# A decode-attention kernel on one core: weight loads in two head halves, K/V transfers in pairs, softmax statistics in a ring

## The chip, the cores and the metric

The kernel runs on one core of one Trainium2 chip. The metric is the device time of one execution in microseconds (us). Runs of one kernel agree within about 1%; all runs quoted here are fast (none lies over 1.5% above the fastest of its kernel). A ratio is the mean time of one kernel's fast runs over the mean of the other's fast runs of the same rounds, so it is not quite the ratio of the medians that are quoted beside it.

Engines: PE is the matmul engine (PEld its weight loads), DVE the vector engine, ACT the scalar engine, POOL the GpSimd engine, SP the engine that issues DMA.

## The reference

Two independent attention blocks, A and B, each one decode step against its own cache; the outputs are joined. bf16 throughout.

```python
# B=8 sequences, D=1024, H=32 heads, Sk=4096 cached keys, Dh=128; twice, for A and B
q = (x @ wq).reshape(B, 1, H, Dh).transpose(0, 2, 1, 3)
scores = einsum("bhqd,bhkd->bhqk", q, k_cache) * Dh ** -0.5
p = softmax(scores, axis=-1)
o = einsum("bhqk,bhkd->bhqd", p, v_cache)
out = o.transpose(0, 2, 1, 3).reshape(B, 1, H * Dh) @ wo
```

2 x 8 x 32 = 512 pairs of cache and head are 512 *units*. Each needs 1 MB of K and 1 MB of V; with the weights, 1107 MB are read.

## The kernel before

Every operation is recorded in a graph (engine, emitter, dependencies, guessed duration, priority). A greedy list scheduler then fixes one order for each engine, in its own model of time:

```python
def _schedule(ops, cfg):
    SEM_LAT = cfg.get("sem_lat", 0.15)
    DMA_US_PER_MB = cfg.get("dma_us_per_mb", 2.72)
    ...                                  # among the operations that are ready, on all engines:
                key = (st, op.prio, op.idx, st)   # earliest modelled start, then priority
```

In a quarter of the units ("P") PE transposes K and does the scores; in the others ("D") DVE multiplies, adds and reduces. After the scores every unit goes through the same softmax chain:

```python
            o1 = g.add("dve", lambda e: e.tensor_reduce(rmax[:, u:u + 1], src, AX.X, ALU.max), [opScore[u]], 0.22, f"rmax{u}", prio - 0.5)
            o2 = g.add("pool", lambda e: e.partition_all_reduce(gmax[:, u:u + 1], rmax[:, u:u + 1], 128, bass.bass_isa.ReduceOp.max),
                       [o1], 0.45, f"armax{u}", prio)
            o3 = g.add("pool", lambda e: e.tensor_scalar(negb[:, u:u + 1], gmax[:, u:u + 1], -scale, None, ALU.mult),
                       [o2], 0.22, f"negb{u}", prio)
            o4 = g.add("act", lambda e: e.activation(pT[:, u % PR, :], src, ACTF.Exp, bias=negb[:, u:u + 1],
                                                     scale=scale, accum_out=rsum[:, u:u + 1]),
                       [o3, opPV.get(u - PR)], 0.42, f"exp{u}", prio - 0.5)
            ...
            if b == B - 1:               # last unit of a head: add the sums over the partitions
                opAradd[(c, h)] = g.add("pool", lambda e, ua0=ua0: e.partition_all_reduce(Lall[:, ua0:u + 1], rsum[:, ua0:u + 1], 128, bass.bass_isa.ReduceOp.add), ...)
```

I call the all-reduce of the maximum **G**, the tiny scale after it **n**, and the all-reduce of a head's sums **L**. All three run on POOL. Note that the model prices G at 0.45 us and n at 0.22 us.

The K, V and weight transfers:

```python
            opK[u] = dma(K_sb[:, kslot, :], caches[c][1][b, h].rearrange("(m t) d -> m (t d)", t=T), ("k", kslot), [opKfree.get(u - NK)], ...)
            opV[u] = dma(V_sb[:, vslot, :], caches[c][2][b, h].rearrange("(m t) d -> m (t d)", t=T), ("v", vslot), [opPV.get(u - NV)], ...)
        ...
        W_sb = sb("W_sb", [128, WSZ], BF16)      # WSZ = max(DC * HD, H * D): a whole weight matrix
```

## Time and profile before

| | before |
|---|---|
| time, median of 16 runs | 8114.6 us (8095 to 8135) |
| profiled span | 8100.5 us |
| time per unit | 15.8 us |
| busiest engine | DVE, 29% |
| DMA | 36% of 16 engines, 137 GB/s |

First the page of the kernel before: busy time with the share of the span, and the DMA queue with packets, MB and share.

```profile
PE 2257.7 (28%) x11890; PEld 940.4 (12%) x11890; DVE 2309.2 (29%) x1833; ACT 1035.8 (13%) x1893; POOL 614.6 (8%) x1106
...
q1 hardware_dynamic: 158272, 1107.43, 35.6%
...
issue 66%; DVE 17%; PE 8%; POOL 5%; ACT 2%; POOLq 0%; DMA 0%; SPq 0%; DVEq 0%
```

Nothing is busy even a third of the time, and two thirds of the chain that ended last are "issue": time in which an engine waited for nothing that the profile shows. So look for who waits, not for who works. The table of waits of the kernel before (engine, line and tile, what released it; us in total, times, longest):

```profile
ACT pT L419 <- POOL negb L417: 5810.5, 480, 21.9
PEld sc L435 <- ACT pT L419: 5110.6, 359, 32.2
...
POOL negb L417 <- issue: 4314.1, 479, 12.2
...
POOL gmax L415 <- issue: 1756.1, 289, 11.1
...
DVE prod L393 <- ACT qbc L552: 42.8, 18, 12.0
```

The exponential waits for n, PE waits for the exponential, and POOL, the engine with the least work, waits for "issue" in front of n and G. DVE's multiply waits 42.8 us in all, and that for qbc, not for K. The serial chain on POOL sets the pace; the question is what POOL does in those gaps. The views by source line of the kernel before answer it (op and count; duration in ns min/median/max; first and last start):

```profile
L417 POOLq MODIFY_POOL_CONFIG  x958: 82/83/83, 46.4 to 8081.5; - x192
L417 POOL TENSOR_SCALAR negb<-gmax x512: 209/261/2248, 56.8 to 8088.8; 128x1 f32<-128x1 f32 x171
...
L415 POOLq MODIFY_POOL_CONFIG  x832: 11/11/11, 14.6 to 8074.7; - x167
L415 POOL PARTITION_ALL_REDUCE gmax<-rmax x512: 352/379/2490, 45.2 to 8081.1; - x171
...
L426 POOLq MODIFY_POOL_CONFIG  x128: 11/11/11, 168.1 to 8089.4; - x128
```

What the trace shows is two MODIFY_POOL_CONFIG records in front of every change from G or L to n or back, and none between two instructions of one kind (G and L count as one kind). 958 records are 479 changes before n, 832 are 416 before G (one of them ahead of the first G), 128 are 64 before L. The records are 11 or 83 ns long; the time is in the gap behind them, never under 5.4 us in this trace. I call such a change, with its records and its gap, a *swap*; the recorded texts call it a reload. What POOL does in the gap is shown by no trace here. The timeline of POOL alone shows the rhythm (start, duration, instruction, and in brackets the idle time before it):

```profile
4054.68 0.26 POOL L417 TENSOR_SCALAR negb<-gmax 128x1 f32<-128x1 f32 x1 [9.17 <-issue]
4060.82 0.38 POOL L415 PARTITION_ALL_REDUCE gmax<-rmax  x1 [5.89 <-issue]
4068.41 0.26 POOL L417 TENSOR_SCALAR negb<-gmax 128x1 f32<-128x1 f32 x1 [7.21 <-issue]
4074.71 0.38 POOL L415 PARTITION_ALL_REDUCE gmax<-rmax  x1 [6.03 <-issue]
```

From start to start that is 6.1 and 6.3 us from n to G and 7.6 us from G to n, for instructions that report 0.26 and 0.38 us. So I time POOL from start to start.

### The profile page before, as it was taken

How to read it: one execution, taken by the hardware profiler on the slowest of the kernel's cores; microseconds unless marked ns; L12 is line 12 of the kernel's file. 1: busy time of each engine (PE TensorE's matmuls, PEld its weight loads, DVE VectorE, ACT ScalarE, POOL GpSimd, SP SyncE). 2: the span in 40 equal slices, each digit the busy share in tenths (PEclk: the TensorE clock that was granted, in tenths of full speed). 3: DMA queues.
4: the chain of work that ended last, by engine and by line, in shares of the span. 5: the costliest groups of instructions: out<-in, count | busy, mean ns of one | idle time of the engine just before them, and what ended most of it. 6: DMA issues, size and time to landing. Idle time of an engine off the chain costs nothing.

```text
span 8100.5 us, 32499 instructions
## 1 busy us (share of the span) xinstructions
PE 2257.7 (28%) x11890; PEld 940.4 (12%) x11890; DVE 2309.2 (29%) x1833; ACT 1035.8 (13%) x1893; POOL 614.6 (8%) x1106
## 2 busy tenths in 40 slices
PE   2222322222222222222222223222232222222223
PEld 1111111111111111111101111111111111111111
DVE  3232322323232233232222323223233232232322
ACT  1011111111111111111111111111111111111111
POOL 0000000000000000000000000000000000000000
PEclk7565565656556665656656665555565666566566
DMA  5433433333333333333343334333343333333332
GB/s 236 177 126 131 156 123 128 134 135 145 120 140 125 135 151 119 145 115 144 146 156 135 125 135 156 124 126 134 124 156 125 135 125 142 138 125 135 125 145 88
DMA packets 158431, 1109.50 MB, mean 137 GB/s; under 512 B 16928, under 2 KB 16928, under 8 KB 25152
## 3 DMA queue, kind: packets, MB, share of 16 engines
q1 hardware_dynamic: 158272, 1107.43, 35.6%
q8 instruction: 94, 1.54, 0.1%
q14 instruction: 65, 0.53, 0.0%
HBM read 1107.33 MB, written 0.03 MB: 137 GB/s over the span
## 4 chain that ended last, share of the span: by engine, by line
issue 66%; DVE 17%; PE 8%; POOL 5%; ACT 2%; POOLq 0%; DMA 0%; SPq 0%; DVEq 0%
DVE prod L393 7%; DVE s_sb L409 7%; PE sc L435 6%; POOL gmax L415 4%; DVE prod L403 3%; POOL negb L417 1%; PE sc L378 1%; ACT pT L419 1%; DVE rmax L414 1%; ACT KT_sb L367 1%; ACT accS L444 1%; PE misc L514 0%; POOLq L417 0%; PE kt_all L357 0%; POOL Lall L426 0%
## 5 line engine op out<-in xcount | busy, mean ns | idle before, releaser
L435 PE MATMUL sc<-V_sb,pT 128*4 128x512 bf16 x4096 | 1654.8, 577 | 5377.8 <-ACT pT L419 4962.7
L435 PEld LDWEIGHTS sc<-V_sb,pT 128*4 128x4 bf16 x4096 | 414.2, 111 | 6372.7 <-ACT pT L419 5110.6
L409 DVE TENSOR_REDUCE s_sb<-prod 128x32 f32<-128x2048 bf16 x382 | 872.8, 2285 | 719.1 <-ACT pT L419 708.6
L393 DVE TENSOR_TENSOR prod<-K_sb,qbc 128x4096 bf16<-128x4096 bf16 x382 | 871.7, 2282 | 42.8 <-ACT qbc L552 42.8
L414 DVE TENSOR_REDUCE rmax<-sc 128x1 f32<-128x32 f32 x130 | 24.7, 190 | 2612.2 <-PE sc L378 2612.2
L495 DVE RECIPROCAL rl<-Lall 128x8 f32<-128x8 f32 x64 | 13.0, 203 | 2261.3 <-POOL Lall L426 2261.3
L419 ACT ACTIVATE pT<-s_sb,negb 128x32 bf16<-128x32 f32 x382 | 122.7, 321 | 4167.9 <-POOL negb L417 4167.9
L415 POOL PARTITION_ALL_REDUCE gmax<-rmax x512 | 379.9, 747 | 2770.1 <-issue 1756.1
L417 POOL TENSOR_SCALAR negb<-gmax 128x1 f32<-128x1 f32 x512 | 202.2, 395 | 4316.7 <-issue 4314.1
L367 ACT ACTIVATE KT_sb<-kt_all 128x2048 bf16<-128x2048 bf16 x260 | 480.3, 1869 | 124.8 <-PE kt_all L357 124.4
L403 DVE TENSOR_TENSOR prod<-prod 128x2048 bf16<-128x2048 bf16 x382 | 467.8, 1225 | 9.7
L444 ACT ACTIVATE accS<-sc 4x512 bf16<-4x512 f32 x512 | 301.1, 588 | 1052.8 <-PE sc L435 1047.5
L357 PE MATMUL kt_all<-ident,K_sb 128*128 128x128 f32 x2080 | 329.3, 315 | 0.0
L357 PEld LDWEIGHTS kt_all<-ident,K_sb 128*128 128x128 f32 x2080 | 278.0, 165 | 119.0 <-issue 119.0
L419 ACT ACTIVATE pT<-sc,negb 128x32 bf16<-128x32 f32 x130 | 37.3, 287 | 1643.1 <-POOL negb L417 1642.7
L378 PE MATMUL sc<-QB,KT_sb 128*128 128x64 bf16 x4160 | 190.2, 215 | 133.1 <-ACT KT_sb L367 132.2
L378 PEld LDWEIGHTS sc<-QB,KT_sb 128*128 128x128 bf16 x4160 | 173.0, 113 | 206.3 <-ACT KT_sb L367 168.6
L452 PE MATMUL o_ps<-E,accS 128*128 128x4 bf16 x512 | 33.2, 169 | 185.9 <-ACT accS L444 185.8
L414 DVE TENSOR_REDUCE rmax<-s_sb 128x1 f32<-128x32 f32 x382 | 68.8, 180 | 10.6
L419 ACT ACTIVATION_READ_ACCUMULATOR pT<-s_sb,negb 128x1 f32 x382 | 71.1, 186 | 0.0
L552 ACT ACTIVATE qbc<-misc 128x512 bf16<-128x512 f32 x96 | 56.9, 593 | 69.2 <-PE misc L545 56.8
L545 PE MATMUL misc<-ident,qT_sb 128*128 128x128 bf16 x382 | 44.9, 251 | 57.8 <-ACT qbc L552 43.2
(39 smaller groups left out, 233.7 us busy)
## 6 DMA issues: line engine op xcount, KB each, us to landing
K_sb<-in_A_k_cache_dram SPq DMA_DIRECT2D x256, 1024.0 KB, 6.9
V_sb<-in_A_v_cache_dram SPq DMA_DIRECT2D x256, 1024.0 KB, 4.8
K_sb<-in_B_k_cache_dram SPq DMA_DIRECT2D x256, 1024.0 KB, 6.9
V_sb<-in_B_v_cache_dram SPq DMA_DIRECT2D x256, 1024.0 KB, 4.8
W_sb<-in_A_wq_dram SPq DMA_DIRECT2D x8, 1024.0 KB, 12.0
W_sb<-in_B_wq_dram SPq DMA_DIRECT2D x8, 1024.0 KB, 13.7
W_sb<-in_A_wo_dram SPq DMA_DIRECT2D x8, 1024.0 KB, 13.6
W_sb<-in_B_wo_dram SPq DMA_DIRECT2D x8, 1024.0 KB, 13.7
```

The source lines that it names most:

```text
L357: last = e.transpose(kt_all[:, gg, tt * 128:(tt + 1) * 128], K32[:, kslot, tp * 128:(tp + 1) * 128], ident32[:])
L367: return e.activation(KT_sb[:, pi % 2, lo * 1024:hi * 1024], ktb_all[:, lo:hi, :].rearrange("p g c -> p (g c)"), ACTF.Copy)
L378: last = e.matmul(bank[:, 2 * tp:2 * tp + MW], KT_sb[:, pi % 2, tp * 256 + e_:(tp + 1) * 256:2], QB[:, c, (j * 2 + e_) * 2:(j * 2 + e_) * ...
L393: lambda e: e.tensor_tensor(pv_, K_sb[:, kslot, :].rearrange("p (t d) -> p t d", d=Dh), qbc[:, gi % 2, i, :].unsqueeze(1).to_broadcast([12 ...
L403: lambda e, width=width: e.tensor_tensor(pv_[:, :, 0:width], pv_[:, :, 0:width], pv_[:, :, width:2 * width], ALU.add),
L409: lambda e, width=width: e.tensor_reduce(s_sb[:, di % SR, :], pv_[:, :, 0:width], AX.X, ALU.add),
L414: o1 = g.add("dve", lambda e: e.tensor_reduce(rmax[:, u:u + 1], src, AX.X, ALU.max), [opScore[u]], 0.22, f"rmax{u}", prio - 0.5)
L415: o2 = g.add("pool", lambda e: e.partition_all_reduce(gmax[:, u:u + 1], rmax[:, u:u + 1], 128, bass.bass_isa.ReduceOp.max), [o1], 0.45, f" ...
L417: o3 = g.add("pool", lambda e: e.tensor_scalar(negb[:, u:u + 1], gmax[:, u:u + 1], -scale, None, ALU.mult), [o2], 0.22, f"negb{u}", prio)
L419: o4 = g.add("act", lambda e: e.activation(pT[:, u % PR, :], src, ACTF.Exp, bias=negb[:, u:u + 1], scale=scale, accum_out=rsum[:, u:u + 1] ...
L435: last = e.matmul(pbank[32 * q4:32 * q4 + 4, 0:512], pT[:, u % PR, 4 * gq:4 * gq + 4], V_sb[:, vslot, gq * 512:(gq + 1) * 512], start=(gq ...
L444: opAcc[u] = g.add("act", lambda e: e.activation(accS[32 * q4:32 * q4 + 4, ring, :], pbank[32 * q4:32 * q4 + 4, 0:512], ACTF.Copy), [opPV[ ...
```

## The change

The intent is about data movement: load each weight matrix in two halves by heads, so that the weight buffer shrinks by half; spend the memory on deeper rings of buffers that are filled in turn (K 8 slots for 5, V 6 for 5); bring K and V of two units in one 2 MB transfer; keep the softmax statistics in a ring of 64 columns rather than one column a unit. No arithmetic changes. The core of the diff:

```diff
-    NK = cfg.get("NK", 5)
-    NV = cfg.get("NV", 5)
+    NK = cfg.get("NK", 8)
+    NV = cfg.get("NV", 6)
...
-    WSZ = max(DC * HD, H * D)
+    WH = cfg.get("w_parts", 2)
+    HP = H // WH
+    WSZ = max(DC * HP * Dh, HP * D)
...
+            if op.dma_key == "w" and op.slack > 0:
+                op.done += W_EXTRA                 # the model: weights land 25 us later
...
-            opK[u] = dma(K_sb[:, kslot, :], caches[c][1][b, h].rearrange("(m t) d -> m (t d)", t=T),
-                         ("k", kslot), [opKfree.get(u - NK)], f"K{u}", MB, prio)
+            if PAIR and u < NT - cfg.get("tail_unpaired", 4):
+                if u % 2 == 0:
+                    opK[u] = opK[u + 1] = dma(
+                        K_sb[:, kslot:kslot + 2, :], caches[c][1][b:b + 2, h].rearrange("u (m t) d -> m u (t d)", t=T),
+                        ("k", kslot), [opKfree.get(u - NK), opKfree.get(u + 1 - NK)], f"K{u}", 2 * MB, prio)
...                                              # V likewise
-        rmax = sb("rmax", [128, NT], FP32)
+        rmax = sb("rmax", [128, RS], FP32)         # RS = 64; gmax, negb, rsum, Lall likewise
...
-            o2 = g.add("pool", lambda e: e.partition_all_reduce(gmax[:, u:u + 1], rmax[:, u:u + 1], 128, bass.bass_isa.ReduceOp.max),
-                       [o1], 0.45, f"armax{u}", prio)
+            o2 = g.add("pool", lambda e: e.partition_all_reduce(gmax[:, ur:ur + 1], rmax[:, ur:ur + 1], 128, bass.bass_isa.ReduceOp.max),
+                       [o1, opNegb.get(u - RS)], 0.45, f"armax{u}", prio)
```

The diff touches POOL only to rename columns and to add waits on work that lies 64 units back. But the order of POOL's instructions comes out of the scheduler, and the scheduler's picture of when K arrives has changed. Before predicting, I built both kernels and compared the orders that the scheduler made.

More of the change, by code (lines that the diff above doesn't have):

```diff
@@ L53, in _schedule @@
     DMA_MARGIN = cfg.get("dma_margin", 5.0)
+    W_EXTRA = cfg.get("w_extra", 25.0)
     for i, op in enumerate(ops):
@@ L132, in _build_kernel @@
     kinds_pat = cfg.get("kinds", "PDDD")
+    PAIR = cfg.get("pair", True)
+    if PAIR:
+        assert NK % 2 == 0 and NV % 2 == 0
     x0, k0, v0, wq0, wo0 = caches[0]
@@ L146, in _build_kernel @@
     scale = float(Dh) ** -0.5
-    WSZ = max(DC * HD, H * D)
+    WH = cfg.get("w_parts", 2)
+    assert H % WH == 0
+    HP = H // WH
+    WSZ = max(DC * HP * Dh, HP * D)
     PW = min(512, D)
@@ L172, in _build_kernel @@
         E4 = sb("E4", [128, 4, 4], BF16)
-        QB = sb("QB", [128, NC, 4 * N + MW], BF16)
+        QB = sb("QB", [128, NC * WH, 4 * HP * B + MW], BF16)
         accS = sb("accS", [128, AR, 512], BF16)
@@ L184, in _build_kernel @@
         s_sb = sb("s_sb", [128, SR, T], FP32)
-        rmax = sb("rmax", [128, NT], FP32)
-        gmax = sb("gmax", [128, NT], FP32)
-        negb = sb("negb", [128, NT], FP32)
-        rsum = sb("rsum", [128, NT], FP32)
-        Lall = sb("Lall", [128, NT], FP32)
+        RS = min(NT, cfg.get("stat_ring", 64))
+        assert RS % B == 0 and RS >= 4 * B
+        rmax = sb("rmax", [128, RS], FP32)
+        gmax = sb("gmax", [128, RS], FP32)
+        negb = sb("negb", [128, RS], FP32)
+        rsum = sb("rsum", [128, RS], FP32)
+        Lall = sb("Lall", [128, RS], FP32)
         pT = sb("pT", [128, PR, T], BF16)
@@ L254, in _build_kernel, with load_wq @@
         misc_last = [None]
-        def load_wq(c, prio):
+        def load_wq(c, part, prio):
             ops = []
+            wcols = HP * Dh
             for dc in range(DC):
-                ops.append(dma(W_sb[:, dc * HD:(dc + 1) * HD], caches[c][3][dc * 128:(dc + 1) * 128, :],
-                               "w", [W_last[0]], f"wq{c}_{dc}", 128 * HD * 2, prio + 0.01 * dc))
+                ops.append(dma(W_sb[:, dc * wcols:(dc + 1) * wcols],
+                               caches[c][3][dc * 128:(dc + 1) * 128, part * wcols:(part + 1) * wcols],
+                               "w", [W_last[0]], f"wq{c}_{part}_{dc}", 128 * wcols * 2, prio + 0.01 * dc))
                 if W_last[0] is not None:
@@ L263, in load_wq, with load_wo @@
             return ops
-        def load_wo(c, prio):
+        def load_wo(c, part, prio):
             ops = []
-            hs = 4 if H % 4 == 0 else 1
-            for h0 in range(0, H, hs):
+            hs = 4 if HP % 4 == 0 else 1
+            for h0 in range(0, HP, hs):
+                hg = part * HP + h0
                 ops.append(dma(W_sb[:, h0 * D:(h0 + hs) * D].rearrange("p (h n) -> p h n", h=hs),
-                               caches[c][4][h0 * 128:(h0 + hs) * 128, :].rearrange("(h p) n -> p h n", p=128),
-                               "w", [W_last[0]], f"wo{c}_{h0}", 128 * hs * D * 2, prio + 0.01 * h0))
+                               caches[c][4][hg * 128:(hg + hs) * 128, :].rearrange("(h p) n -> p h n", p=128),
+                               "w", [W_last[0]], f"wo{c}_{part}_{h0}", 128 * hs * D * 2, prio + 0.01 * h0))
                 if W_last[0] is not None:
@@ L285, in _build_kernel, with q_compute @@
         misc_last[0] = op_xT
-        op_q = [None] * NC
-        def q_compute(c, wq_ops, prio):
+        op_q = {}
+        op_qT = {}
+        def q_compute(c, part, wq_ops, prio):
+            wcols = HP * Dh
+            j0, j1 = part * HP * B, (part + 1) * HP * B
+            n = j1 - j0
             def emit_q(e):
                 last = None
-                for h in range(H):
+                for hl in range(HP):
                     for dc in range(DC):
-                        last = e.matmul(misc[:, h * B:(h + 1) * B],
-                                        W_sb[:, dc * HD + h * 128: dc * HD + (h + 1) * 128],
+                        last = e.matmul(misc[:, hl * B:(hl + 1) * B],
+                                        W_sb[:, dc * wcols + hl * 128: dc * wcols + (hl + 1) * 128],
                                         xT_sb[:, (c * DC + dc) * B:(c * DC + dc + 1) * B],
@@ L298, in emit_q @@
                 return last
-            qm = g.add("pe", emit_q, [op_xT, misc_last[0]] + wq_ops, 0.03 * H * DC, f"q{c}", prio)
+            qm = g.add("pe", emit_q, [op_xT, misc_last[0]] + wq_ops, 0.03 * HP * DC, f"q{c}_{part}", prio)
             W_last[0] = qm
-            ev = g.add("dve", lambda e: e.tensor_copy(qT_sb[:, c, 0:N], misc[:, 0:N]), [qm], 1.3, f"q{c}_evac", prio)
+            ev = g.add("dve", lambda e: e.tensor_copy(qT_sb[:, c, j0:j1], misc[:, 0:n]), [qm], 0.3 + n / 256.0, f"q{c}_{part}_evac", prio)
             def emit_perm(e):
-                e.matmul(misc[:, 0:N], selA[:], qT_sb[:, c, 0:N], start=True, stop=True)
-                return e.matmul(misc[:, N:2 * N], selB[:], qT_sb[:, c, 0:N], start=True, stop=True)
-            pm = g.add("pe", emit_perm, [ev] + sel_ops, 0.6, f"q{c}_perm", prio)
-            QBv = QB[:, c, 0:4 * N].rearrange("p (j e n) -> p j e n", e=2, n=2)
+                e.matmul(misc[:, 0:n], selA[:], qT_sb[:, c, j0:j1], start=True, stop=True)
+                return e.matmul(misc[:, n:2 * n], selB[:], qT_sb[:, c, j0:j1], start=True, stop=True)
+            pm = g.add("pe", emit_perm, [ev] + sel_ops, 0.4, f"q{c}_{part}_perm", prio)
+            QBv = QB[:, c * WH + part, 0:4 * n].rearrange("p (j e n) -> p j e n", e=2, n=2)
             def emit_cp(e):
-                e.tensor_copy(QBv[0:64, :, 0, 0], misc[0:64, 0:N])
-                e.tensor_copy(QBv[64:128, :, 1, 1], misc[64:128, 0:N])
-                e.tensor_copy(QBv[0:64, :, 1, 0], misc[0:64, N:2 * N])
-                return e.tensor_copy(QBv[64:128, :, 0, 1], misc[64:128, N:2 * N])
-            cp = g.add("dve", emit_cp, [pm, op_zQB], 3.0, f"q{c}_cp", prio)
+                e.tensor_copy(QBv[0:64, :, 0, 0], misc[0:64, 0:n])
+                e.tensor_copy(QBv[64:128, :, 1, 1], misc[64:128, 0:n])
+                e.tensor_copy(QBv[0:64, :, 1, 0], misc[0:64, n:2 * n])
+                return e.tensor_copy(QBv[64:128, :, 0, 1], misc[64:128, n:2 * n])
+            cp = g.add("dve", emit_cp, [pm, op_zQB], 0.8 + 2.2 * n / 256.0, f"q{c}_{part}_cp", prio)
             misc_last[0] = cp
-            op_q[c] = cp
-            return ev, cp
+            op_q[(c, part)] = cp
+            op_qT[(c, part)] = ev
         def unit_src(u):
@@ L325, in _build_kernel @@
         opEvac, opQK, opRed = {}, {}, {}
+        opArmax, opNegb, opHEa = {}, {}, {}
         opExt = {}
@@ L328, in _build_kernel @@
         opHE = {}
-        op_qT = [None] * NC
         opQbc = {}
@@ L337, in make_unit @@
             prio = float(u)
-            opK[u] = dma(K_sb[:, kslot, :], caches[c][1][b, h].rearrange("(m t) d -> m (t d)", t=T),
-                         ("k", kslot), [opKfree.get(u - NK)], f"K{u}", MB, prio)
-            opV[u] = dma(V_sb[:, vslot, :], caches[c][2][b, h].rearrange("(m t) d -> m (t d)", t=T),
-                         ("v", vslot), [opPV.get(u - NV)], f"V{u}", MB, prio + cfg.get("v_prio", 2.5))
+            if PAIR and u < NT - cfg.get("tail_unpaired", 4):
[3 more added lines that the diff above has]
+                        ("k", kslot), [opKfree.get(u - NK), opKfree.get(u + 1 - NK)], f"K{u}", 2 * MB, prio)
+                    opV[u] = opV[u + 1] = dma(
+                        V_sb[:, vslot:vslot + 2, :], caches[c][2][b:b + 2, h].rearrange("u (m t) d -> m u (t d)", t=T),
+                        ("v", vslot), [opPV.get(u - NV), opPV.get(u + 1 - NV)], f"V{u}", 2 * MB, prio + cfg.get("v_prio", 2.5))
+            else:
+                opK[u] = dma(K_sb[:, kslot, :], caches[c][1][b, h].rearrange("(m t) d -> m (t d)", t=T),
+                             ("k", kslot), [opKfree.get(u - NK)], f"K{u}", MB, prio)
+                opV[u] = dma(V_sb[:, vslot, :], caches[c][2][b, h].rearrange("(m t) d -> m (t d)", t=T),
+                             ("v", vslot), [opPV.get(u - NV)], f"V{u}", MB, prio + cfg.get("v_prio", 2.5))
             if kind[u] == "P":
@@ L372, in make_unit @@
                 bank = sc[0]
+                qpart = h // HP
+                jl = j - qpart * HP * B
                 def emit_QK(e):
@@ L379, in emit_QK @@
                                             KT_sb[:, pi % 2, tp * 256 + e_:(tp + 1) * 256:2],
-                                            QB[:, c, (j * 2 + e_) * 2:(j * 2 + e_) * 2 + MW],
+                                            QB[:, c * WH + qpart, (jl * 2 + e_) * 2:(jl * 2 + e_) * 2 + MW],
                                             start=(e_ == 0), stop=(e_ == 1))
                     return last
-                opQK[u] = g.add("pe", emit_QK, evs + [op_q[c], opExp.get(prevP)], 1.0, f"QK{u}", prio)
+                opQK[u] = g.add("pe", emit_QK, evs + [op_q[(c, h // HP)], opExp.get(prevP)], 1.0, f"QK{u}", prio)
                 opScore[u] = opQK[u]
@@ L413, in make_unit @@
                 src = s_sb[:, di % SR, :]
-            o1 = g.add("dve", lambda e: e.tensor_reduce(rmax[:, u:u + 1], src, AX.X, ALU.max), [opScore[u]], 0.22, f"rmax{u}", prio - 0.5)
-            o2 = g.add("pool", lambda e: e.partition_all_reduce(gmax[:, u:u + 1], rmax[:, u:u + 1], 128, bass.bass_isa.ReduceOp.max),
-                       [o1], 0.45, f"armax{u}", prio)
-            o3 = g.add("pool", lambda e: e.tensor_scalar(negb[:, u:u + 1], gmax[:, u:u + 1], -scale, None, ALU.mult),
-                       [o2], 0.22, f"negb{u}", prio)
-            o4 = g.add("act", lambda e: e.activation(pT[:, u % PR, :], src, ACTF.Exp, bias=negb[:, u:u + 1],
-                                                     scale=scale, accum_out=rsum[:, u:u + 1]),
-                       [o3, opPV.get(u - PR)], 0.42, f"exp{u}", prio - 0.5)
+            ur = u % RS
+            old_head = ((u - RS) // N, ((u - RS) % N) // B) if u >= RS else None
+            o1 = g.add("dve", lambda e: e.tensor_reduce(rmax[:, ur:ur + 1], src, AX.X, ALU.max),
+                       [opScore[u], opArmax.get(u - RS)], 0.22, f"rmax{u}", prio - 0.5)
+            o2 = g.add("pool", lambda e: e.partition_all_reduce(gmax[:, ur:ur + 1], rmax[:, ur:ur + 1], 128, bass.bass_isa.ReduceOp.max),
+                       [o1, opNegb.get(u - RS)], 0.45, f"armax{u}", prio)
+            opArmax[u] = o2
+            o3 = g.add("pool", lambda e: e.tensor_scalar(negb[:, ur:ur + 1], gmax[:, ur:ur + 1], -scale, None, ALU.mult),
+                       [o2, opExp.get(u - RS)], 0.22, f"negb{u}", prio)
+            opNegb[u] = o3
+            o4 = g.add("act", lambda e: e.activation(pT[:, u % PR, :], src, ACTF.Exp, bias=negb[:, ur:ur + 1],
+                                                     scale=scale, accum_out=rsum[:, ur:ur + 1]),
+                       [o3, opPV.get(u - PR), opAradd.get(old_head) if old_head else None], 0.42, f"exp{u}", prio - 0.5)
             opExp[u] = o4
@@ L424, in make_unit @@
                 ua0 = u - (B - 1)
+                ur0 = ua0 % RS
                 opAradd[(c, h)] = g.add(
-                    "pool", lambda e, ua0=ua0: e.partition_all_reduce(Lall[:, ua0:u + 1], rsum[:, ua0:u + 1], 128, bass.bass_isa.ReduceOp.add),
-                    [opExp[uu] for uu in range(ua0, u + 1)], 0.5, f"aradd{c}_{h}", prio)
+                    "pool", lambda e, ur0=ur0: e.partition_all_reduce(Lall[:, ur0:ur0 + B], rsum[:, ur0:ur0 + B], 128, bass.bass_isa.ReduceOp.add),
+                    [opExp[uu] for uu in range(ua0, u + 1)] + [opHEa.get(old_head) if old_head else None], 0.5, f"aradd{c}_{h}", prio)
             q4 = u % 4
@@ L475, in piece_sizes @@
             sizes = []
-            rem = H
-            while rem > 5:
-                sizes.append(4)
-                rem -= 4
-            if rem > 1:
-                sizes.append(rem - 1)
-            sizes.append(1)
+            for part in range(WH):
+                rem = HP
+                lastpart = (part == WH - 1)
+                while rem > (5 if lastpart else 4):
+                    sizes.append(4)
+                    rem -= 4
+                if lastpart:
+                    if rem > 1:
+                        sizes.append(rem - 1)
+                    sizes.append(1)
+                elif rem:
+                    sizes.append(rem)
             return sizes
         PSZ = piece_sizes()
+        assert sum(PSZ) == H
         PEND = []
@@ L494, in make_head @@
             ring = h % 4
-            a = g.add("dve", lambda e: e.reciprocal(rl[:, ring, :], Lall[:, u0:u0 + B]),
+            ur0 = u0 % RS
+            a = g.add("dve", lambda e: e.reciprocal(rl[:, ring, :], Lall[:, ur0:ur0 + B]),
                       [opAradd[(c, h)], opHE.get((c, h - 4))], 0.2, f"HEa{c}_{h}", prio - 0.4)
+            opHEa[(c, h)] = a
             lastgrp = (u0 + B - 1) // 4
@@ L507, in make_piece @@
             final = (h1 == H)
-            if c not in wo_ops:
-                wo_ops[c] = load_wo(c, prio - cfg.get("wo_ahead", 40.0) if h0 == 0 else prio)
+            part = h0 // HP
+            assert (h1 - 1) // HP == part
+            if (c, part) not in wo_ops:
+                assert len(op_q) == NC * WH
+                wo_ops[(c, part)] = load_wo(c, part, prio - cfg.get("wo_ahead", 40.0))
             for ph in range(NPH):
@@ L513, in emit_P @@
                     for hh in range(h0, h1):
-                        last = e.matmul(misc[0:B, 0:PW], on_sb[:, c, hh, :], W_sb[:, hh * D + ph * PW: hh * D + (ph + 1) * PW],
+                        hl = hh - part * HP
+                        last = e.matmul(misc[0:B, 0:PW], on_sb[:, c, hh, :], W_sb[:, hl * D + ph * PW: hl * D + (ph + 1) * PW],
                                         start=(hh == h0), stop=(hh == h1 - 1))
                     return last
-                pm = g.add("pe", emit_P, [opHE[(c, hh)] for hh in range(h0, h1)] + [misc_last[0]] + wo_ops[c],
+                pm = g.add("pe", emit_P, [opHE[(c, hh)] for hh in range(h0, h1)] + [misc_last[0]] + wo_ops[(c, part)],
                            0.23 * (h1 - h0), f"P{c}_{h0}_{ph}", prio - 0.4)
@@ L520, in make_piece @@
                 if h0 == 0:
-                    ev = g.add("dve", lambda e, dst=dst: e.tensor_copy(dst, misc[0:B, 0:PW]), [pm], 0.7, f"Pev{c}_{h0}_{ph}", prio - 0.4)
+                    ev = g.add("dve", lambda e, dst=dst: e.tensor_copy(dst, misc[0:B, 0:PW]),
+                               [pm], 0.7, f"Pev{c}_{h0}_{ph}", prio - 0.4)
                 else:
@@ L526, in make_piece @@
                 misc_last[0] = ev
-                if final and ph == NPH - 1:
+                if (h1 % HP == 0) and ph == NPH - 1:
                     W_last[0] = pm
@@ L547, in emit_qb @@
                 return last
-            qdeps = [op_qT[cc] for cc in sorted(set(uu // N for uu in units))]
-            assert all(q_ is not None for q_ in qdeps)
+            qdeps = [op_qT[k_] for k_ in sorted(set((uu // N, ((uu % N) // B) // HP) for uu in units))]
             qm = g.add("pe", emit_qb, [misc_last[0], op_ident] + qdeps, 0.06 * n, f"qbc{gi}", prio)
@@ L556, in make_qbc @@
             opQbc[gi] = ev
-        wq0 = load_wq(0, -50.0)
-        ev0, _ = q_compute(0, wq0, -50.0)
-        op_qT[0] = ev0
-        Q_AT = {c: cfg.get("q_at", min(24, N // 4)) * c for c in range(1, NC)}
-        qbc_groups_done = set()
-        for u in range(NT):
-            c = u // N
-            for cc in range(1, NC):
-                if u == Q_AT[cc]:
-                    wqs = load_wq(cc, float(u) - 8.0)
-                    ev_, _ = q_compute(cc, wqs, float(u))
-                    op_qT[cc] = ev_
+        q_sched = [(c, part) for c in range(NC) for part in range(WH)]
+        first_piece_unit = PSZ[0] * B - 1
+        Q_STEP = max(1, (first_piece_unit - 1) // len(q_sched))
+        assert (len(q_sched) - 1) * Q_STEP < first_piece_unit
+        q_at = {}
+        for i, (c, part) in enumerate(q_sched):
+            q_at[(c, part)] = i * Q_STEP
+        wqs = load_wq(0, 0, -50.0)
+        q_compute(0, 0, wqs, -50.0)
+        for u in range(NT):
+            for (c_, part) in q_sched[1:]:
+                if u == q_at[(c_, part)]:
+                    wqs = load_wq(c_, part, float(u) - 6.0)
+                    q_compute(c_, part, wqs, float(u))
             if kind[u] == "D" and d_index[u] % 4 == 0:
```

## The prediction

> **What bounds the kernel now.** No engine is busy: DVE 29%, PE 28%, ACT 13%, POOL 8%, DMA 36% (busy table, queue table). The chain of waits is 66% "issue", and the waits table says where: POOL before `negb` sits idle 4314 us (479 times) and before `gmax` 2770 us, mostly released by nothing but issue. ACT's exp waits 5811 us for `negb`; PE's PV waits for exp. So POOL's serial chain sets the time: all-reduce (G), scale (n), 512 units, 15.8 us each.
>
> [...]the view of line 417 holds 958 MODIFY_POOL_CONFIG records (two per reload: 479), line 415 832 (416), line 426 128 (64). [...]n to next G, start to start, has a minimum of 5.99 and a median of 6.29 us; without a reload between (n to n) it is 0.34. G to n with a reload: median 9.5, range 7.0 to 13.9. Against the bytes that DMA started meanwhile, G to n fits 7.34 us + 1.2 us/MB (mean 2.0 MB), n to G 6.3 + 1.24 us/MB. So a round trip costs 13.64 us plus a DMA share that follows the bytes, about 1260 us in all. Check: 479 x 13.64 = 6533, + 1260, + about 223 for G after the per-head sum all-reduce (L), + 28 + 11 for G-G and n-n, + 45 before the first G = 8100.
>
> **What the change does.** Half-size weight loads, paired K/V transfers, deeper rings and a ring of statistics change no arithmetic and no bytes, and DMA at 36% is not the limit. K is not waited for (DVE's multiply waits 43 us in all, for qbc). The intent itself is worth little: the first weight load halves, so the first G comes perhaps 12 us sooner than 45 us. The ring's waits lie 64 units back.
>
> But the kernel's static scheduler reorders POOL. Built, the order has 448 reloads before `negb` instead of 479, 386 instead of 416 before `gmax`, 63 instead of 64 before the sum: adjacent G-G pairs rise from 33 to 64, each saving a round trip. That is -31 x 13.64 = -423 us, all critical. Second: before, 13 of 63 L-G transitions have HEb, two projection evictions and one multiply-add-reduce on DVE between the head's reciprocal and the maximum that G needs (about 12 us each in the trace); after, about 5. Rest 0.8 us. Gain: about 110 us. Back: some 37 us for more G-G and n-n.
>
> 8100 - 423 - 110 - 12 + 37 = 7592; as timed, 7600.
>
> **Prediction: 7600 us, 7470 to 7770.** Faster by over 2%: 0.95; within 2%: 0.04; slower: 0.01.
>
> **What would show it.** POOL reloads about 897 pairs of records in place of 959; n to G still 6.3, G to n still 7.34 at no bytes; L to G mostly 0.8. Busy PE, DVE, ACT and MB moved unchanged.
>
> **What would make it wrong.** Longer bursts (4 MB per two units) may delay a reload more per MB than 1.2 us. The SP queue may block behind a weight load that waits for PE, so that DVE waits for K. The second G of a pair may wait for a maximum that isn't ready.

The sum comes to 7592 us, and its 13.64 us for a round trip is 7.34 and 6.3 us, the two constants fitted to the trace.

## The result, and the profile after

| | before | after |
|---|---|---|
| median | 8114.6 us (16 runs) | 7624.1 us (8 runs, 7608 to 7634) |
| ratio of fast runs | | 0.9394, 95% interval 0.9381 to 0.9407 |
| profiled span | 8100.5 us | 7628.6 us |
| swaps before n / G / L | 479 / 416 / 64 | 448 / 386 / 63 |

The page and the waits of the changed kernel; the lines answer to those shown above.

```profile
PE 2295.0 (30%) x11894; PEld 927.7 (12%) x11894; DVE 2310.9 (30%) x1843; ACT 1032.2 (14%) x1893; POOL 555.2 (7%) x1106
...
q1 hardware_dynamic: 152448, 1107.40, 36.8%
...
issue 69%; DVE 14%; PE 6%; POOL 6%; ACT 3%; POOLq 1%; DMA 0%; SPq 0%; DVEq 0%; ACTq 0%
```

```profile
ACT pT L454 <- POOL negb L451: 5202.5, 450, 20.8
POOL negb L451 <- issue: 4116.1, 448, 13.8
...
POOL gmax L448 <- issue: 1623.2, 263, 12.7
```

The same picture, a little shorter: the bytes are equal, DVE and ACT worked as long as before, and the chain is still "issue". What fell is the number of gaps, 479 to 448 before n. The views by source line of the changed kernel count the swaps:

```profile
L451 POOLq MODIFY_POOL_CONFIG  x896: 82/83/108, 30.1 to 7609.4; - x180
...
L448 POOLq MODIFY_POOL_CONFIG  x772: 11/11/11, 15.1 to 7602.7; - x193
...
L462 POOLq MODIFY_POOL_CONFIG  x126: 11/11/11, 150.7 to 7617.2; - x126
```

And POOL's timeline in the changed kernel shows what a saved round trip looks like. The "x2" are two all-reduces side by side and then two scales side by side, with one swap between them instead of three:

```profile
4047.86 0.43 POOL L462 PARTITION_ALL_REDUCE Lall<-rsum  x1 [6.02 <-issue]
4048.69 3.66 POOL L448 PARTITION_ALL_REDUCE gmax<-rmax  x2 [0.40 <-DVE rmax L446]
4062.59 1.61 POOL L451 TENSOR_SCALAR negb<-gmax 128x1 f32<-128x1 f32 x2 [10.25 <-issue]
```

POOL's time can be added up without a remainder from starts to starts (worked out from the two traces, us):

| | before | after | change | predicted |
|---|---|---|---|---|
| steps with a swap: G to n, n to G, n to L, L to n | 7787 | 7430 | -357 | -423 |
| L to G | 224 (63) | 101 (62) | -123 | -110 |
| G to G and n to n | 39 (66) | 62 (128) | +23 | +37 |
| before the first G | 45.2 | 29.7 | -15 | -12 |

The four changes add up to -472 us, the difference of the spans.

### The profile page after: what moved, and what is told of

It reads as the page before. It is cut to its first block, busy times and chain, and to the rows that moved or that the text cites. A ratio compares the mean times of both kernels' runs of the same rounds, so it can differ in the third digit from the quotient of the medians.

```text
span 7628.6 us, 31653 instructions
## 1 busy us (share of the span) xinstructions
PE 2295.0 (30%) x11894; PEld 927.7 (12%) x11894; DVE 2310.9 (30%) x1843; ACT 1032.2 (14%) x1893; POOL 555.2 (7%) x1106
## 4 chain that ended last, share of the span: by engine, by line
issue 69%; DVE 14%; PE 6%; POOL 6%; ACT 3%; POOLq 1%; DMA 0%; SPq 0%; DVEq 0%; ACTq 0%
DVE s_sb L439 6%; DVE prod L423 5%; PE sc L471 4%; POOL gmax L448 4%; DVE prod L433 2%; POOL negb L451 2%; ACT pT L454 1%; PE sc L408 1%; ACT KT_sb L395 1%; ACT accS L480 1%; DVE rmax L446 1%; PE misc L562 1%; POOLq L451 0%; PE kt_all L385 0%; POOL Lall L462 0%
## 5 line engine op out<-in xcount | busy, mean ns | idle before, releaser
L471 PE MATMUL sc<-V_sb,pT 128*4 128x512 bf16 x4096 | 1689.3, 587 | 4495.5 <-ACT pT L454 3941.4
L423 DVE TENSOR_TENSOR prod<-K_sb,qbc 128x4096 bf16<-128x4096 bf16 x382 | 872.0, 2283 | 51.2 <-ACT qbc L600 51.2
L448 POOL PARTITION_ALL_REDUCE gmax<-rmax x512 | 359.2, 712 | 2559.7 <-issue 1623.2
L451 POOL TENSOR_SCALAR negb<-gmax 128x1 f32<-128x1 f32 x512 | 163.0, 318 | 4121.2 <-issue 4116.1
L385 PE MATMUL kt_all<-ident,K_sb 128*128 128x128 f32 x2080 | 311.0, 308 | 0.5 <-DMA K_sb<-in_A_k_cache_dram 0.5
L488 PEld LDWEIGHTS o_ps<-E,accS 128*128 128x128 bf16 x512 | 24.8, 105 | 550.3 <-ACT accS L480 549.7
```

The lines of the kernel that those rows point to most:

```text
L385: last = e.transpose(kt_all[:, gg, tt * 128:(tt + 1) * 128], K32[:, kslot, tp * 128:(tp + 1) * 128], ident32[:])
L423: lambda e: e.tensor_tensor(pv_, K_sb[:, kslot, :].rearrange("p (t d) -> p t d", d=Dh), qbc[:, gi % 2, i, :].unsqueeze(1).to_broadcast([12 ...
L451: o3 = g.add("pool", lambda e: e.tensor_scalar(negb[:, ur:ur + 1], gmax[:, ur:ur + 1], -scale, None, ALU.mult), [o2, opExp.get(u - RS)], 0 ...
L471: last = e.matmul(pbank[32 * q4:32 * q4 + 4, 0:512], pT[:, u % PR, 4 * gq:4 * gq + 4], V_sb[:, vslot, gq * 512:(gq + 1) * 512], start=(gq ...
```

## The experiments

All were run in three rounds beside the kernel before (8125 to 8137 us in these rounds). "Theory" is the one above: the swaps set the time. Runs 1 to 5, 9 and 12 test it; the others share the gain out and size the terms.

### 1. The same order, transfers not merged

```diff
-    opK[u] = opK[u + 1] = dma(K_sb[:, kslot:kslot + 2, :], caches[c][1][b:b + 2, h]..., 2 * MB, prio)
+    opK[u] = opK[u + 1] = dma2([(K_sb[:, kslot + i, :], caches[c][1][b + i, h]...) for i in range(2)], ..., 2 * MB, prio)
     # V likewise; one graph operation issues two transfers, each raising the same semaphore
```

> The changed kernel with every 2 MB K/V transfer issued as two 1 MB transfers at the same place in the queue, on the same semaphore; the order of instructions on every engine is that of the changed kernel (compared name by name), so POOL has the same 448 round trips of reloads. Theory (reload count sets the time): the changed kernel's time, 7624 us within 60. Rival (fewer, larger K/V transfers made it faster): back towards 8114 us, at least to 7850.

Measured: 7677.7 us, ratio to before 0.9437 (0.9414 to 0.9460). All engines' orders are those of the changed kernel, and 93% of the gain by the ratios (0.0563 of 0.0606) is there with 1 MB transfers. Larger transfers can account for about the difference of the two ratios, 0.4% of the time before.

### 2. All the transfers of the change, but no two all-reduces side by side

```diff
-                       [o1, opNegb.get(u - RS)], 0.45, f"armax{u}", prio)
+                       [o1, opNegb.get(u - RS), opNegb.get(u - 1)], 0.45, f"armax{u}", prio)
```

> The changed kernel with all its transfers and rings, but each all-reduce (G) made to wait for the scale (n) of the unit before it, so that no two G stand side by side: 512 round trips of reloads instead of 448. Theory: 512 x 13.64 + 1260 for the bytes + about 140 for start, end and the per-head sums = about 8390 us (8300 to 8650), slower than the kernel before although every transfer is the changed kernel's. Rival (paired transfers, smaller weight loads, deeper rings made it faster): about 7624 us, at most 7750.

Measured: 8493.9 us, ratio 1.0444 (1.0412 to 1.0476). With paired transfers, half weight loads and deep rings all in place, the kernel is slower than the one before, as soon as POOL has to swap 512 times. The rival falls here.

### 3 and 4. No swap at all: the scale moves to ACT

The same edit on both kernels:

```diff
-            o3 = g.add("pool", lambda e: e.tensor_scalar(negb[...], gmax[...], -scale, None, ALU.mult),
+            o3 = g.add("act", lambda e: e.activation(negb[...], gmax[...], ACTF.Copy, scale=-scale),
```

> The kernel before with the 128x1 scale (n) moved from POOL to ACT, so POOL runs all-reduces alone[...]. Theory (the idle time of POOL is reloading): the round trips vanish, and the next limit is DMA (1109 MB busy 36.8% of 7629 us = about 2810 us) or DVE (2310 us busy): 3000 to 3800 us. Rival (the all-reduce itself runs about 14 us, and the profile doesn't show it): within 5% of 8114 us.

> The changed kernel with the scale (n) moved from POOL to ACT. Theory: 2900 to 3600 us; with no reload in the way, paired transfers and earlier weights can show their own worth, so 0 to 10% under the kernel before with the same edit. Rival (the all-reduce itself is slow): within 5% of 7624 us.

Measured: 2739.6 us for the kernel before with the edit (ratio 0.3365, 0.3355 to 0.3375), 2737.8 us for the changed one with the edit (0.3364, 0.3354 to 0.3374), both correct. Both went below the ranges I had given, and two thirds of the time are gone for one line. The lines of the changed kernel with the scale on ACT: its busy line and DMA queue from the page, and a line of its waits.

```profile
PE 1784.1 (65%) x11894; PEld 814.8 (30%) x11894; DVE 2306.4 (84%) x1843; ACT 1111.3 (41%) x2405; POOL 1003.4 (37%) x594
...
q1 hardware_dynamic: 152448, 1107.40, 98.3%
```

```profile
POOL gmax L448 <- DVE rmax L446: 1630.5, 423, 19.0
```

POOL now waits for DVE, that is for work, and DMA is busy 98% of the span at a mean of 406 GB/s. The fullest slices of its page reach 421 to 422 GB/s. (The chain that ended last names DVE first, 40%, and DMA for 10% only: that DMA is now the limit is read from its busy share and was not tested.) So the all-reduce itself was never slow: the view by line of the same run, with 512 of them and one swap at the start, has

```profile
L448 POOL PARTITION_ALL_REDUCE gmax<-rmax x512: 350/2316/2477, 29.3 to 2719.2; - x171
L448 POOLq MODIFY_POOL_CONFIG  x2: 11/11/11, 15.2 to 15.2; - x2
```

And the point about the change: where DMA, whose transfers it rearranges, is busy 98% of the span (run 4), the two kernels' medians differ by less than 0.1%, within the noise (each ratio is known to 0.3%). Its intended effect is worth nothing measurable even there.

### 5. The kernel before, strictly alternating

```diff
-                       [o1], 0.45, f"armax{u}", prio)
+                       [o1, opNegb.get(u - 1)], 0.45, f"armax{u}", prio)
```

> The kernel before with each all-reduce (G) made to wait for the scale (n) of the unit before it: 512 round trips instead of 479. Theory: 512 x 13.64 + 1260 + about 80 for start, end and per-head sums = about 8325 us (8250 to 8600); and within 2% of the changed kernel with the same edit, since at equal round trips transfers and rings are worth little. Rival: the changed kernel's transfers are worth their 6% here too, so this is 6% above the changed kernel with the same edit.

Measured: 8418.1 us, ratio 1.0372 (1.0339 to 1.0404): by the ratios 0.7% below the changed kernel with the same edit. At equal numbers of round trips the changed transfers bring no gain.

### 6 and 7. One part of the change alone

```diff
-    _build_kernel(nc, caches, out, cfg or {})
+    _build_kernel(nc, caches, out, dict(w_parts=1, NK=6, NV=4, pair=True, stat_ring=512, w_extra=0.0))    # 6: pairs only
+    _build_kernel(nc, caches, out, dict(w_parts=2, NK=5, NV=5, pair=False, stat_ring=512))                # 7: half weights only
```

> Of the change only the pairing of K/V transfers (K ring 6, V ring 4; whole weight loads; full statistics). The built order has 446 reloads to the scale instead of 479 (changed kernel 448), and 3 long L to G waits instead of 13. Theory: 446 x 13.64 + 1260 + 130 for waits and start + the 59 us that the changed kernel lay over the same sum = about 7600 us (7520 to 7700), all of the gain. Rival (deeper rings or half weight loads carry the gain): at least 7850 us.

> Of the change only the half-size weight loads and their extra scheduling slack (rings of 5, K/V one by one, full statistics). The built order has 475 reloads to the scale instead of 479. Theory: 475 x 13.64 + 1260 + about 280 for waits and start = about 8020 us (7950 to 8090). Rival (weight loads carry the gain): at most 7800 us.

Measured: pairs only 7496.3 us, ratio 0.9234 (0.9209 to 0.9259); half weight loads only 8011.8 us, 0.9874 (0.9845 to 0.9903). Pairing carries the whole gain, through the order that it makes the scheduler choose. Run 6 also changes the rings to 6 and 4, and these were not run without pairing. Built without pairing, and not timed, they give 483 swaps before n, and the whole change without pairing gives 469 (before 479, changed 448): the rings alone don't make the order. The statistics ring was not run alone: built alone on the old settings it leaves the count of swaps at 479. Pairs only came out 24 us below the range that I gave, 128 us faster than the whole change with two round trips fewer. Most of it lies in G to n, 9.58 us on average for 9.90; see run 11.

### 8 and 10. What slows a swap: fewer bytes

After the rings' first filling, transfers bring one eighth of each slot; results are wrong, instructions and their order are the same.

```diff
+                    vw = T * Dh if u < NV else 512
-                        V_sb[:, vslot:vslot + 2, :], caches[c][2][b:b + 2, h].rearrange(...),
+                        V_sb[:, vslot:vslot + 2, 0:vw], caches[c][2][b:b + 2, h].rearrange(...)[:, :, 0:vw],
     # run 10: K likewise
```

> The changed kernel, wrong on purpose: from the seventh unit on, each V transfer brings only one eighth of its columns (the rest of the slot keeps old values), so about 460 MB less is moved, in the same order of instructions. Theory (a reload is slowed by transfers running beside it, about 1.1 us per MB): about 7624 - 507 = 7120 us (7020 to 7250), with G to n near 8.8 us on average instead of 9.9 and the same 448 round trips. Rival ([...]bytes don't matter): 7624 us within 60.

> The changed kernel, wrong on purpose: after the rings' first filling both K and V transfers bring one eighth of their columns, same order of instructions; some 920 MB less is moved. It asks what the 1260 us beyond 13.64 us per round trip are. If they are transfers that run beside a reload: 448 x 13.64 + about 330 = 6300 to 6500 us. [...]The run with less V alone gave -339 us for 460 MB, so a straight line would give about 6950 us.

Measured: less V 7285.5 us (461 MB less, -339 us), 35 us above the range that I gave; less V and K 6766.6 us (919 MB less, -857 us), above what transfers alone would give (6300 to 6500). G to n fell from 9.90 us to 9.15 and 8.04. So bytes do slow a swap, by 0.7 to 0.9 us per MB taken out of the run, not by the 1.2 of my fit; and some 8.0 us remain with hardly any bytes (0.26 MB a step). The second candidate in both runs was that DVE holds POOL back; in run 10 it was put at 6700 us or more. In that run the slow ones among these steps do go with DVE: 93 of 447 took 8.5 to 11 us and had about 3 us of DVE's multiply inside, the other steps 0.6 us. The slow steps lift the mean by 0.36 us, so DVE could explain only a part of what remains. Run 4, which swaps once, at its start, shows the two engines side by side:

```profile
1304.67 2.28 DVE L423 TENSOR_TENSOR prod<-K_sb,qbc 128x4096 bf16<-128x4096 bf16 x1
1304.85 2.32 POOL L448 PARTITION_ALL_REDUCE gmax<-rmax  x1 [3.68 <-DVE rmax L446]
...
1314.25 2.29 DVE L439 TENSOR_REDUCE s_sb<-prod 128x32 f32<-128x2048 bf16 x1
1314.41 0.35 POOL L448 PARTITION_ALL_REDUCE gmax<-rmax  x1 [1.24 <-DVE rmax L446]
```

The all-reduce that starts just after DVE's multiply ends 0.22 us after it; beside DVE's reduction it takes 0.35 us. In the whole run the 446 all-reduces that overlap a multiplication of DVE have a median of 2.32 us, the 66 that overlap none 0.35. Why was not shown: no run isolated a reason.

### 9. Half of the round trips

The scale of an even unit waits for the all-reduce of the odd one after it: POOL runs G G n n.

```diff
-                       [o1, opNegb.get(u - RS)], 0.45, f"armax{u}", prio)
+                       [o1, opNegb.get(u - RS), opNegb.get(u // 2 * 2 - 1)], 0.45, f"armax{u}", prio)
+            if u % 2 and u < NT - 2:
+                opNegb[u - 1].deps.append(o2)
```

> The changed kernel with the scale of each even unit made to wait for the all-reduce of the odd unit after it, and the next all-reduce for that pair's second scale: POOL runs G G n n. The built order has 258 reloads to the scale instead of 448. Theory (each round trip costs 13.64 us and the bytes of all transfers cost some 1260 us whatever the count): 258 x 13.64 + 1260 + about 370 for the second members, per-head sums, start and end = about 5150 us (4950 to 5600). Rival (transfers set the time): about 7624 us. If time per round trip grows as trips get fewer, it lies above 5600.

Measured: 5360.1 us, ratio 0.6595 (0.6570 to 0.6620). 190 round trips fewer took off 2264 us, although the second members of pairs cost 438 us more (from the traces); so a round trip was worth (2264 + 438) / 190 = 14.2 us. My first try at this edit did not build: the last two units share one score bank, and their pair would have waited for itself.

### 11. The rings of run 6, half weights kept

```diff
+    _build_kernel(nc, caches, out, dict(NK=6, NV=4))
```

> The changed kernel with K ring 6 and V ring 4 (those of the run that pairs only) in place of 8 and 6; half weight loads kept. The built order has 440 round trips instead of 448 and 2 L to G waits that hold other work instead of 6. By the count alone: 7624 - 8 x 13.64 - 40 = about 7475 us. If the deeper rings are also why the changed kernel's G to n is 0.3 us longer on average than that of the run that pairs only: about 7340 us. If the half weight loads are why: 7475 us.

Measured: 7443.1 us, ratio 0.9147 (0.9128 to 0.9166). The count alone comes nearest. G to n did fall to 9.57 us, but n to G rose from 6.75 to 7.05: shallower rings moved transfers from beside one swap to beside the other (0.43 MB in an n to G for 0.27), and 14 of these steps, for 10, held a head's end (see below), with a small net gain. The deeper rings of the change bought nothing.

### 12. The suspected cost put back alone

To run 4 (no swaps, 2738 us) an idle instruction is added that forces them. It reads a constant, and nothing reads it.

```diff
-  lambda e: e.partition_all_reduce(gmax[...], rmax[...], 128, bass.bass_isa.ReduceOp.max),
+  lambda e: (e.tensor_scalar(dmy[:, u:u + 1], dsrc[:], -scale, None, ALU.mult),
+             e.partition_all_reduce(gmax[...], rmax[...], 128, bass.bass_isa.ReduceOp.max))[1],
```

> The changed kernel with the scale on ACT (POOL without reloads, 2738 us), plus one idle tensor_scalar per unit on POOL just ahead of each all-reduce: 128x1, from a constant tile to a tile that nothing reads; it depends on no all-reduce and nothing depends on it. The built order has 512 reloads before it and 512 before the all-reduce again, where the kernel without it had one. Theory[...]: 512 x 13.64 + 1260 + about 100 = about 8340 us (7800 to 8600). Rival (the cost was the scale's wait for the all-reduce's result, or the order that the scale imposed): near 2738 us, at most 3000.

Measured: 8425.4 us, ratio 1.0375 (1.0330 to 1.0420). The view by line of this run:

```profile
L451 POOLq MODIFY_POOL_CONFIG  x1022: 82/83/108, 36.8 to 8388.5; - x171
L451 POOL TENSOR_SCALAR dmy<-dsrc x512: 260/260/2333, 29.7 to 8395.9; 128x1 f32<-128x1 f32 x171
```

512 instructions that do nothing of use, 0.26 us in the median by the profile, cost 5688 us. Neither n's wait for G nor the order it imposes is needed for the cost; an instruction whose only effect is to force the swap is enough.

## Why the prediction was right

- **The bound.** Right, and shown from four sides: taking the swaps away (runs 3 and 4), putting them back alone (12), more of them (2, 5), fewer of them (9). In the trace before, n to G takes 5.99 us at least and 6.29 in the median; n to n, without a swap, 0.34.
- **What the change does.** Right: the gain is the scheduler's new order, not the transfers. Equal order with small transfers keeps it (1), the new transfers without the order lose it (2), pairing alone carries it (6), and where DMA is busy 98% of the span the change is worth under 0.1% (3 against 4). Why pairing yields more G-G neighbours was seen in the built order only: pairs of a D unit followed by a P unit rose from 4 to 29. That two units become ready together in the scheduler's model, because their K lands together there, is my reading and was not tested.
- **The sum.** 7592 us as a span against 7628.6. The steps with a swap fell by 357 us and not by 423. The missing 66 us are not in the swaps but in the second term, "Gain: about 110 us". The prediction was right that the work at a head's end (HEb and two projection evictions on DVE) leaves L to G: 13 such steps before, 5 after. It did not ask where this work goes. Eight of the heads' ends moved one step on, into the n to G that follows, where G waits for a maximum behind them. One of these in the changed kernel, DVE and POOL:

```profile
2501.11 0.26 POOL L451 TENSOR_SCALAR negb<-gmax 128x1 f32<-128x1 f32 x1 [8.77 <-issue]
2504.96 0.67 DVE L572 TENSOR_TENSOR oacc<-oacc,misc 8x512 f32<-8x512 f32 x1 [1.96 <-PE misc L562]
2507.59 0.67 DVE L572 TENSOR_TENSOR oacc<-oacc,misc 8x512 f32<-8x512 f32 x1 [1.96 <-PE misc L562]
...
2515.57 0.18 DVE L446 TENSOR_REDUCE rmax<-s_sb 128x1 f32<-128x32 f32 x1
2515.89 2.31 POOL L448 PARTITION_ALL_REDUCE gmax<-rmax  x1 [14.52 <-DVE rmax L446]
```

The trace before has 2 such n to G, the one after 10, of 14.8 us each for 6.5 in the other n to G: eight times 8.3 us is 66 us. So the second term was worth about 57 us (123 - 66) and not 110. The swaps themselves came as predicted: what G to n took beyond 7.34 us adds up to 1151 us before and 1147 after, so the bytes kept their share although they fall on fewer swaps (2.13 MB in a G to n for 2.00). The split behind that share is less sharp than "13.64 us" and "1260 us" say: by runs 8 and 10 bytes cost 0.7 to 0.9 us per MB, and a round trip nearly without them about 14.7 us (8.04 + 6.65). The other terms came out 3 to 14 us better than predicted each, 30 us together; that they hide half of the miss is luck.
- **The warnings.** None of the three hurt much. The SP queue did stand behind a weight load that waited for PE, for 47.3 us at the longest (until 5796.8 us of the changed kernel; the V transfer behind it, which had nothing of its own to wait for, started at 5799.2), but DVE's multiply waited there for qbc alone, 51.2 us in all. The second G of a pair started 0.63 us after the first on average. It was the G behind a head's end that waited, as above. Longer bursts did not cost more per MB in the fit (1.07 us per MB after, 1.2 before); the part of a G to n without bytes rose in it from 7.34 to 7.62 us, where the prediction had it unchanged.

What stays open: how ring depth decides beside which swap the bursts fall (run 6 is 128 us faster than the change; two round trips, 27 us, and L to G, 28, less the later start, 15, explain 40 of them; run 11 is 181 us faster, and eight round trips, 109, and L to G, 39, explain 148), and how much of the 8.04 us goes with DVE's multiply (about 0.36 us by the slow steps of run 10, if all of these are DVE's).

The version to keep is run 4, or run 3 with the simpler code: a third of the time.

## What to carry to other kernels

When no engine is busy and the chain is mostly "issue", look for configuration records on the engine whose product everybody waits for, and time it from start to start; two tiny instructions of different kinds in turn cost more here than all the mathematics: 16.3 us a round trip on average in the kernel before (9.74 from G to n, 6.55 from n to G), and 8115 us in all where run 3, the same kernel with a single swap, needs 2740. Before crediting a change with its intent, compare the order of instructions it produces: here a change of transfers won 6% by accidentally grouping POOL's work, and a scheduler that priced a swap at nothing had hidden a factor of three. When a wait leaves one step, ask in which step it turns up again: eight of the heads' ends here only moved on by one. And move the odd instruction to another engine (run 4, 2738 us) rather than group it (run 9, 5360 us).
